# A gated recurrence and a low-rank mixer on one core: another order of the work from the fourth chunk on

## The chip, the cores and the metric

The kernel runs on one core of one Trainium2 chip. The metric is the device time of one execution in microseconds (us). "PE" is TensorE, "PEld" its weight loads, "DVE" VectorE, "ACT" ScalarE, "POOL" GpSimd and "SP" SyncE, which here only starts transfers (DMAs).

## The reference, cut to what matters

The input is q, k, v and a complex gate (a_re, a_im) for 4 batches of 8 heads, 768 steps and 48 channels. A complex state of 48x48 per head is decayed by the gate and takes in the outer product of k and v at each step; q reads its real part. The result, as 768 rows of 384, goes through a mixer over the steps of rank 32 and a two-layer mixer over the channels.

```python
for t in range(S):
    S_re, S_im = ar * S_re - ai * S_im + outer(k[t], v[t]), ar * S_im + ai * S_re
    y[t] = q[t] @ S_re
...
h = x.T @ U @ V
u = x + h.T
out = u + np.maximum(u @ w_ch1, 0.0) @ w_ch2
```

## The kernel before

**Tiles and stages.** Time is cut into chunks of 128 steps: 6 per batch, 24 in all, numbered 0 to 23. Two neighbouring chunks make a group (12 groups). Each chunk goes through these steps, and the names are those of the code and of the profile:

- *gates* (magnitudes, within, totals; L640 to L758): logarithms and exponentials of the gate's size on ACT and DVE, running sums of them on PE ("es ps", "ef ps" at L699 or L705, "tot" at L745 or L751).
- *angles* (turns, waves; L761 to L842): the gate's phase, its running sum on PE ("ph", L806 to L814), sine and cosine ("cs") on ACT.
- *prep* (L850 to L893): DVE multiplies q and k with sizes and phases ("QKC", 768 elements a row), PE transposes them ("tr", L873), ACT copies the result to "QK".
- *levels* (L895 to L972): products of q and k inside the chunk on PE ("inner", first at L923, then the near ones at L920), with scalings of QK on DVE between (L397 is the shared multiply) and masked copies to "DG" (L935). SP then places DG into "AT" by four transfers per chunk (L971).
- *rest* (L973 to L1060): "corners" (L984), the chunk's own key-value product "dk" (L1009), the carried state "G" and "GM" on DVE, and the outputs "y" (L1040 for the part inside the chunk, which reads AT; L1048 for the carried state), copied by ACT to "xo".
- *mixer* (from L1064): for every two chunks of a finished batch, "rank", "mixed", "uTp", then the two layers. The first three pairs use "up" (L1135), later ones "few" (L1235), a scheme with fewer products that needs sums on DVE (L1247, L400); "down" (L1326 and L1369) is the second layer. These are the long products; those of levels and rest are short.

**What sets the order.** The code first records all operations with `plan.add`: the engine, a rank (a stage and a number), what is read and written, and the buffers that are held. Nothing is issued then. Class `Plan`, method `order`, looks up a place in one list for each recorded operation in the table `ORDER`, under its engine and rank, sorts by place, and the operations are then issued in that order. Each engine, and SP's queue too, runs its own operations strictly in this order. Between operations of different engines the list decides nothing: there the semaphores of what is read and written, and of buffers that come free, decide.

Two further tables go with it. `BANKS` holds one letter for each tile in PSUM, in the order in which the tiles are recorded: it names one of four pools ("psT", "psA", "psY", "psM"), each with two buffers. `SPARE` says after which places products without use are issued, each of 128 columns (function `idle`, L1528); there are 91, 72 of them ahead of place 360. No search is part of the file: the tables were made outside it.

Of the kernel before, what the change touches and what calls it, by code (L numbers as in the profile page):

```python
# [30 lines left out]
    "TTTTTTTTTTTTTTTTTTAAAAYYYYTTAAAAYYYYTTAAAAYYYYTTAAAAYYYYTTTTTTTTTTAAAAYYYYTTAAAAYYYTTTMMMMMMTTAAYYAATTMMTTTTMMMMMYMMAMAY"  # L31
    "YYTTMYMMTTTTTTTTTTTTTTTTTTAAATYYMTTTAAAYTYTAYTMMYAAAATYTTTYAAAATYYTTMMTATYYTYAMTTYYYYMYTYYAAMAYYAATATTTAMMAAYMMAYATTAYYM"
    "MTMMAYMMTTTMMTTTAAATTATYATTAYATAYMYYATTTYTAYYTTYMATAYMAYAATYTYTMYAATYYMYMMYYYATYATYATAAATTATYAYAYAYTYATYMYATYMYYAYTTTTAA"
    "TTYMMYYYAAYYTYYYAYYTATYTATATMMAYYATMTAMTMYYYTAYYMMYAYAMYYAMMYTATTTYAYATYTATTTTYATMYMTMTMYYMMTTYATYYMYYTYMATTAAYMAMYYAMA")
# [12 lines left out]
        ('POOL', 'load'): {0: [14], 1: [34], 1.5: [84], 2: [31]},  # L47
        ('DVE', 'load'): {1: [58]},
# [6 lines left out]
        ('ACT', 'gates'): {0: [1, 2, 4, 6, 7, 16, 17, 22, 23, 29, 28, 45, 70, 71], 1: [24, 27, 38, 39, 41, 42, 46, 47, 65, 64, 67, 68], 2: [129, 108,  # L55
# [10 lines left out]
        ('DVE', 'gates'): {0: [5, 8, 13, 18, 19, 54, 49], 1: [30, 21, 40, 43, 44, 51, 50], 2: [111, 143, 156, 185, 169], 4: [277, 322, 323, 372, 356],  # L66
# [10 lines left out]
        ('ACT', 'angles'): {0: [72, 86, 98, 100, 103], 1: [76, 106, 112, 114, 126], 2: [210, 231, 251, 240, 241, 242, 263, 269, 271], 4: [375, 395,  # L77
# [5 lines left out]
        ('DVE', 'angles'): {0: [81, 89], 1: [87, 107], 2: [211, 232, 252], 4: [376, 402, 425], 6: [589, 596, 601, 611, 624, 625, 664], 8: [697, 714,  # L83
# [4 lines left out]
        ('DVE', 'prep'): {0: [85, 104, 110], 1: [121, 128, 145], 2: [226, 250, 265], 3: [203, 304, 309], 4: [373, 424, 427], 5: [443, 470, 472], 6:  # L88
# [1509 lines left out]
```

## Time and profile before

| | |
|---|---|
| median of 3 runs | 621.91 us (621.03 to 622.38) |
| profiled execution, its own time | 619.11 us |
| its span (first to last instruction) | 616.9 us |
| TensorE clock granted, mean | 0.997 |
| busy: PE / DVE / ACT / POOL | 598.9 / 531.5 / 401.8 / 36.3 us |
| PE matmul records | 10,572 |
| moved by DMA | 45.77 MB |

The profile is of one execution. Its first table gives each engine's busy time and its share of the span. A view by stretches gives the same for parts of the span. A view of waits tells for how long an engine sat idle before a line and what released it; "issue" is written where no semaphore explains the idle time. The timeline gives start, duration, engine, line and names, with the idle time before a row in square brackets; neighbouring rows of one line are merged, and a merged row ends when its last result is out, so the next row often starts before that.

### The profile page before, as it was taken

How to read it: one execution, taken by the hardware profiler on the slowest of the kernel's cores; microseconds unless marked ns; L12 is line 12 of the kernel's file. 1: busy time of each engine (PE TensorE's matmuls, PEld its weight loads, DVE VectorE, ACT ScalarE, POOL GpSimd, SP SyncE). 2: the span in 40 equal slices, each digit the busy share in tenths (PEclk: the TensorE clock that was granted, in tenths of full speed). 3: DMA queues.
4: the chain of work that ended last, by engine and by line, in shares of the span. 5: the costliest groups of instructions: out<-in, count | busy, mean ns of one | idle time of the engine just before them, and what ended most of it. 6: DMA issues, size and time to landing. Idle time of an engine off the chain costs nothing.

```text
span 616.9 us, 23966 instructions
## 1 busy us (share of the span) xinstructions
PE 598.9 (97%) x10572; PEld 526.8 (85%) x10572; DVE 531.5 (86%) x967; ACT 401.8 (65%) x789; POOL 36.3 (6%) x76
## 2 busy tenths in 40 slices
PE   6998989999999999999999999999999999999998
PEld 3566767656889979899999999899999998999997
DVE  6999999998999999999999999789889986464554
ACT  6999998989888896886696876565652622202020
POOL 4000000000000010000100100000110000000000
PEclk8999999999999999999999999999999999999999
DMA  9865565644233542521523331700122301000000
GB/s 214 198 148 114 136 133 140 157 126 92 50 57 80 92 85 48 109 54 32 113 49 59 86 70 34 137 9 3 39 54 52 65 9 20 21 7 7 20 20 26
DMA packets 173687, 45.77 MB, mean 74 GB/s; under 512 B 167632, under 2 KB 170384, under 8 KB 173584
## 3 DMA queue, kind: packets, MB, share of 16 engines
q1 hardware_dynamic: 171376, 39.90, 31.4%
q0 software_dynamic: 2208, 4.35, 2.1%
q8 instruction: 83, 1.36, 1.0%
q14 instruction: 20, 0.16, 0.1%
HBM read 33.59 MB, written 4.72 MB: 62 GB/s over the span
## 4 chain that ended last, share of the span: by engine, by line
PE 88%; ACT 8%; issue 1%; DVE 1%; DMA 1%; SPq 0%; ACTq 0%
PE down L1369 25%; PE few L1235 20%; PE up L1135 7%; PE dk L1009 4%; PE tr L873 4%; PE y L1048 3%; PE inner L923 3%; PE down L1326 2%; PE inner L920 2%; ACT gate L394 2%; PE y L1040 2%; PE tot L751 2%; PE mixed L1102 2%; PE rank L1083 1%; PE es ps L699 1%; PE up L1528 1%
## 5 line engine op out<-in xcount | busy, mean ns | idle before, releaser
L397 DVE TENSOR_TENSOR QK<-QK,T 96x512 f32<-96x512 f32 (+2 forms) x144 | 102.3, 725 | 1.5 <-PE corners L984 0.9
L1369 PE MATMUL down<-w,h 128*128 128x192 f32 x396 | 72.3, 330 | 0.0
L394 ACT ACTIVATE gate<-gate 128x768 f32<-128x768 f32 (+1 forms) x82 | 64.7, 795 | 9.3 <-DVE GS L801 5.5
L1369 PEld LDWEIGHTS down<-w,h 128*128 128x128 f32 x396 | 64.5, 190 | 1.3 <-issue 0.7
L884 ACT COPY QK<-tr 96x512 f32<-96x512 f32 x96 | 51.0, 587 | 16.9 <-PE tr L873 16.6
L1243 ACT COPY h<-few 128x512 f32<-128x512 f32 x54 | 31.1, 589 | 46.2 <-PE few L1235 34.3
L1135 PE MATMUL up<-uT,w 128*128 128x256 f32 x216 | 50.4, 385 | 0.0
L400 DVE TENSOR_TENSOR xo<-down,xo 128x192 f32<-128x192 f32 (+1 forms) x79 | 30.1, 384 | 23.1 <-PE down L1369 22.7
L1235 PE MATMUL few<-stage,w 128*128 128x128 f32 x360 | 47.1, 277 | 0.0
L1135 PEld LDWEIGHTS up<-uT,w 128*128 128x128 f32 x216 | 39.9, 190 | 5.5
L1235 PEld LDWEIGHTS few<-stage,w 128*128 128x128 f32 x360 | 44.0, 192 | 0.2
L1247 DVE CUSTOM_DVE_ANT_1 h<-few,h 128x512 f32<-128x512 f32 x54 | 35.9, 684 | 8.4 <-PE few L1235 7.0
L397 DVE TENSOR_TENSOR QKC<-qk,cs 128x768 f32<-128x768 f32 x44 | 41.7, 950 | 1.5 <-PE dk L1009 1.1
L989 ACT COPY AT<-corners 32x128 f32<-32x128 f32 x96 | 24.4, 257 | 24.6 <-PE corners L984 23.3
L1235 PE MATMUL few<-stage,sums 128*128 128x128 f32 x288 | 37.8, 278 | 0.0
L1369 PE MATMUL down<-stage 128*128 128x192 f32 x198 | 37.3, 330 | 0.0
L1235 PEld LDWEIGHTS few<-stage,sums 128*128 128x128 f32 x288 | 34.7, 192 | 0.6
L788 POOL DMA_DIRECT2D gate<-F x15 | 12.0, 799 | 362.6 <-DVE w L587 112.5
L1369 PEld LDWEIGHTS down<-stage 128*128 128x128 f32 x198 | 32.2, 190 | 1.0 <-issue 0.6
L873 PEld LDWEIGHTS tr<-ident,QKC 64*96 64x96 f32 x768 | 24.2, 123 | 10.0 <-issue 3.5
L400 DVE TENSOR_TENSOR h<-few,h 128x512 f32<-128x512 f32 x27 | 18.3, 686 | 16.4 <-PE few L1235 12.4
L873 PE MATMUL tr<-ident,QKC 64*96 64x64 f32 x768 | 29.4, 220 | 2.7 <-DVE QKC L397 1.6
(195 smaller groups left out, 1351.2 us busy)
## 6 DMA issues: line engine op xcount, KB each, us to landing
stage<-in_moe_w_ch_dram SPq DMA_DIRECT2D x12, 768.0 KB, 5.0
qk<-in_q_dram SPq DMA_DIRECT2D x24, 192.0 KB, 3.2
qk<-in_k_dram SPq DMA_DIRECT2D x24, 192.0 KB, 3.8
VP<-in_v_dram SPq DMA_DIRECT2D x24, 192.0 KB, 4.1
gate<-in_a_re_dram SPq DMA_DIRECT2D x22, 192.0 KB, 4.1
gate<-in_a_im_dram SPq DMA_DIRECT2D x22, 192.0 KB, 4.1
AT<-DG SPq DMA_DIRECT2D x96, 32.0 KB, 2.0
T<-E SPq DMA_DIRECT2D x48, 48.0 KB, 3.2
```

What stands on the lines that cost most here:

```text
L394: return nc.scalar.activation(out=o, in_=i, func=f, **kw)
L397: nc.vector.tensor_tensor(out=o, in0=a, in1=b, op=OP.mult)
L400: nc.vector.tensor_tensor(out=o, in0=a, in1=b, op=OP.add)
L873: nc.tensor.transpose(out=get(*ps[r])[0:DQ, h], in_=get(*qkc)[at, h * DQ:(h + 1) * DQ], identity=ident[at, at], tile_position=(r * HC, 0))
L884: nc.scalar.copy(out=to, in_=a)
L989: ACT(0.36, RR, lambda r=r, u=u: nc.scalar.copy(out=get(*ATi).rearrange("p (a u) t -> p a u t", u=2)[r:r + BLK, :, u, BLK:2 * BLK], in_=ge ...
L1009: nc.tensor.matmul(out=get(*dk[r])[x:x + w, h], lhsT=get(*ks)[at, h * DQ + x:h * DQ + x + w], rhs=get(*VPi)[at, h], start=True, stop=True, ...
L1135: nc.tensor.matmul(out=get(*ps)[:, e], lhsT=w1[:, f, (ff + e) * 128:(ff + e + 1) * 128], rhs=get(*uT)[:, f], start=(f == 0), stop=(f == KD ...
L1235: nc.tensor.matmul(out=get(*ps)[:, q], lhsT=w()[:, q * 128:(q + 1) * 128], rhs=v[0](), start=(n == 0 and q == 0), stop=True, skip_group_ch ...
L1243: ACT(c_act(n3 * CH) - 0.045, RU, lambda i=i, k=k: nc.scalar.copy(out=at(i, k), in_=get(*ps)), [ps], [o])
L1247: DVE(c_dve(n3 * CH), RU, lambda i=i, k=k: nc.vector._custom_dve(dve_ops.TENSOR_ADD_SAT, out=at(i, k), in0=get(*ps), in1=at(i, k), s0=math ...
L1369: nc.tensor.matmul(out=get(*to)[:, part], lhsT=x(j), rhs=y[:, j], start=(first and j == 0), stop=(j == KH - 1), skip_group_check=not first)
```

## The change

Only the three tables differ; every recorded operation, its cost figures and the code that issues it are the same. `ORDER` gives other places from 363 on (the fourth chunk, number 3, is then in its *levels*), `BANKS` other pools from about the 53rd tile on, and `SPARE` other places from 436 on, with the same number of products: 19 behind place 360, 91 in all. The tables come from a search that was carried on with transfers reckoned longer than before; the figures it used are not in the file. One line of each table:

```diff
-        25.7: [2222, 2302], 26: [2298], 26.7: [2279, 2381], 27: [2446]},
+        25.7: [2233, 2289], 26: [2298], 26.7: [2340, 2351], 27: [2458]},
...
-         1, 352: 2, 436: 1, 595: 2, 600: 1, 605: 3, 623: 1, 631: 3, 645: 1, 652: 1, 663: 1, 693: 1, 694: 1, 715: 1, 716: 2}
+         1, 352: 2, 438: 1, 585: 3, 600: 2, 609: 1, 618: 3, 621: 1, 651: 1, 655: 1, 680: 1, 693: 1, 704: 1, 724: 1, 726: 2}
```

PE's first other row stands where the span before is at 75.1 us. Three places follow, as the programs have them.

**PE around chunk 4.** First before, from the corners of chunk 3 to the first inner products of chunk 4. "tr" of QKC_93 and QKC_95 are q and k of chunk 4; "y" belongs to chunk 3, and "up<-ident" and "tr<-ident 128x128" are spare products.

```order
L984 MATMUL corners<-QK 32x32 x16
L873 MATMUL tr<-ident,QKC_93 96x64 x16
L1040 MATMUL y<-VP_104,AT_111 64x48 x16
L1528 MATMUL up<-ident 128x128
L873 MATMUL tr<-ident,QKC_95 96x64 x16
L1048 MATMUL y<-GM,QK 64x48 x8
L1048 MATMUL y<-G,QK 64x48 x8
L923 MATMUL inner<-QK 32x48 x32
```

The same stretch of PE after the change:

```order
L984 MATMUL corners<-QK 32x32 x16
L814 MATMUL ph<-F,ident 128x384
L1135 MATMUL up<-uT,w_66 128x256 x6
L873 MATMUL tr<-ident,QKC_93 96x64 x16
L1528 MATMUL tr<-ident 128x128
L873 MATMUL tr<-ident,QKC_95 96x64 x16
L1040 MATMUL y<-VP_104,AT_111 64x48 x16
L1048 MATMUL y<-G,QK 64x48 x8
L1048 MATMUL y<-GM,QK 64x48 x8
L923 MATMUL inner<-QK 32x48 x32
```

A long "up" now stands ahead of the transposes. Before, it stood behind the inner products, between the two halves of "dk" of chunk 4; behind those came this (near inner products of chunk 4, transposes of chunk 5, the next "up"):

```order
L920 MATMUL inner<-QK 16x16 x32
L873 MATMUL tr<-ident,QKC_93 96x64 x16
L873 MATMUL tr<-ident,QKC_95 96x64 x16
L1135 MATMUL up<-uT,w_66 128x256 x6
L984 MATMUL corners<-QK 32x32 x16
```

After the change both halves of "dk" stand together, and this follows them:

```order
L873 MATMUL tr<-ident,QKC_93 96x64 x16
L873 MATMUL tr<-ident,QKC_95 96x64 x16
L920 MATMUL inner<-QK 16x16 x32
L1135 MATMUL up<-uT,w_66 128x256 x6
L923 MATMUL inner<-QK 32x48 x32
```

So no long product is left between the transposes of chunk 4 and the near inner products of chunk 4.

**DVE at the same place.** Before, from the first QKC of chunk 4 to the QK that "inner" of chunk 4 reads (the last row, with T_103); "w_66" is work on the weights.

```order
L397 TENSOR_TENSOR QKC_93<-qk,cs 128x768
L817 SCALAR_TENSOR_TENSOR F<-F,ph 128x384
L400 ISA w_66<-w_66,stage 128x1536
L397 TENSOR_TENSOR QKC_95<-qk,cs 128x768
L397 TENSOR_TENSOR QK<-QK,T_102 96x1024
L397 TENSOR_TENSOR qk<-qk,es 128x768
L397 TENSOR_TENSOR QK<-QK,T_103 96x512
```

After the change:

```order
L397 TENSOR_TENSOR QK<-QK,T_102 96x1024
L817 SCALAR_TENSOR_TENSOR F<-F,ph 128x384
L397 TENSOR_TENSOR QKC_93<-qk,cs 128x768
L397 TENSOR_TENSOR QKC_95<-qk,cs 128x768
L589 SCALAR_TENSOR_TENSOR w_66<-stage,w_66 128x768
L397 TENSOR_TENSOR G<-GM,T_102 96x384
L397 TENSOR_TENSOR QKC_95<-QKC_95,gate 128x768
L397 TENSOR_TENSOR QK<-QK,T_103 96x512
```

The scaling of chunk 3's QK (1024) moved ahead of both QKC, "qk" of chunk 5 and one row of weights were done earlier, and the second use of QKC_95 (for "dk") stands ahead of the last row and no more behind it.

**SP's queue at the same place.** Before, the four placements of chunk 3 (AT_111 from DG_112) stand together:

```order
L728 DMA T_103<-E 48x2x128 x2
L606 DMA V<-UV 32x4x192
L728 DMA T_103<-E 48x2x128
L971 DMA AT_111<-DG_112 32x8x32 x4
L541 DMA gate<-in_a_im_dram 128x8x48 x2
```

After the change:

```order
L728 DMA T_103<-E 48x2x128
L971 DMA AT_111<-DG_112 32x8x32
L541 DMA gate<-in_a_im_dram 128x8x48
L971 DMA AT_111<-DG_112 32x8x32 x2
L550 DMA VP_105<-in_v_dram 128x8x48
L971 DMA AT_111<-DG_112 32x8x32
```

The last placement of chunk 3 now stands behind two loads, of a gate and of v. The later chunks are reordered in the same manner, on all engines.

More of the change, by code (lines that the diff above doesn't have):

```diff
@@ L30 @@
 BANKS = (
[L31 to L34, printed above, removed]
+    "TTTTTTTTTTTTTTTTTTAAAAYYYYTTAAAAYYYYTTAAAAYYYYTTAAAATTMTTTTTTTAMYMMAMAAAMYYYYMMYATTMTTMAMYTAMMMAYATMTMMMAYTYAYAMAAMMAYTY"
@@ L37 @@
+    "ATYYTTMMMAYTTTYYYYTTYAYAYAATYMYTAYATMATTYTTYYTMAMYATAYTYAYYAAMYYTTATAYYAYATYYTTAMAMTAATYYTAATMYTYAYYYAATTMAAYYYTMMATTMYA"
+    "YYMAMMMAYYYMMAYYATTAAYTTAAYYYTMMAMTMMTTMATYAAAYTMAATMYMAAMYATYYMAATMTMAMAAMAATMAATAAYTTYYATYATTYAYAAYYYTTMYYTMTMYYTTTATT"
+    "MYMMMTAYMMMTATYYATYTAATTYAAAMMYTAATTATTTTTMATMTAMMAYYYTYYTAMATYYYAATTYTYYTATAATAYAYTATAAYTTYMYAATMTTYYMMATMTYTMAYAAAYTT")
 ORDER = {
[1 row of a table removed]
[1 row of a table added]
         97], 2.6: [176], 3: [33, 77, 80, 95], 3.5: [61, 60], 5.1: [124], 5.6: [171], 5.7: [125, 214], 6: [212], 6.1: [267], 6.6: [321], 6.7: [196,
[7 rows of a table removed]
[7 rows of a table added]
@@ L47 @@
         ('POOL', 'load'): {0: [14], 1: [34], 1.5: [84], 2: [31]},
         ('DVE', 'load'): {1: [58]},
[6 rows of a table removed]
[6 rows of a table added]
         ('ACT', 'gates'): {0: [1, 2, 4, 6, 7, 16, 17, 22, 23, 29, 28, 45, 70, 71], 1: [24, 27, 38, 39, 41, 42, 46, 47, 65, 64, 67, 68], 2: [129, 108,
         109, 94, 130, 131, 132, 142, 139, 146, 172, 164, 165, 166, 179, 183, 184, 190, 205, 206], 4: [284, 218, 236, 290, 286, 295, 306, 317, 316,
[9 rows of a table removed]
-        ('DVE', 'gates'): {0: [5, 8, 13, 18, 19, 54, 49], 1: [30, 21, 40, 43, 44, 51, 50], 2: [111, 143, 156, 185, 169], 4: [277, 322, 323, 372, 356],
[10 rows of a table removed]
@@ L77 @@
-        ('ACT', 'angles'): {0: [72, 86, 98, 100, 103], 1: [76, 106, 112, 114, 126], 2: [210, 231, 251, 240, 241, 242, 263, 269, 271], 4: [375, 395,
[5 rows of a table removed]
-        ('DVE', 'angles'): {0: [81, 89], 1: [87, 107], 2: [211, 232, 252], 4: [376, 402, 425], 6: [589, 596, 601, 611, 624, 625, 664], 8: [697, 714,
[4 rows of a table removed]
-        ('DVE', 'prep'): {0: [85, 104, 110], 1: [121, 128, 145], 2: [226, 250, 265], 3: [203, 304, 309], 4: [373, 424, 427], 5: [443, 470, 472], 6:
[6 rows of a table removed]
-        ('ACT', 'prep'): {0: [115, 117, 120, 122], 1: [158, 147, 154, 160], 2: [266, 270, 283, 281], 3: [319, 320, 327, 318], 4: [442, 439, 446, 445],
[4 rows of a table removed]
@@ L100 @@
-        ('DVE', 'rest'): {0: [118, 149, 155, 175, 159, 170, 194], 1: [174, 229, 234, 259, 209, 235, 248, 253], 2: [288, 315, 325, 366, 291, 314, 324,
[8 rows of a table removed]
-        ('DVE', 'levels'): {0: [123, 135, 148, 136, 137, 152], 1: [177, 192, 202, 195, 198, 225], 2: [292, 302, 308, 301, 303, 312], 3: [328, 371,
[9 rows of a table removed]
-        ('ACT', 'levels'): {0: [138], 1: [215], 2: [305], 3: [378], 4: [468], 5: [530], 6: [764], 7: [830], 8: [962], 9: [1058], 10: [1175], 11:
[14 rows of a table removed]
-        ('ACT', 'rest'): {0: [191, 182, 200, 201, 219, 223, 222], 1: [255, 261, 256, 258, 280, 279, 278], 2: [342, 341, 336, 335, 385, 390, 391], 3:
[10 rows of a table removed]
@@ L145 @@
-        ('ACT', 'small'): {0: [594, 285, 307, 492, 396, 554, 590, 549, 622, 635], 1: [742, 800, 775, 808, 780, 844, 860], 2: [900, 930, 1065, 1076,
[4 rows of a table removed]
-        ('DVE', 'small'): {0: [246, 599, 630, 636, 639, 637, 684, 681, 602, 606, 729, 735], 1: [703, 739, 689, 832, 877, 897, 862, 919, 901, 938, 978,
[29 rows of a table removed]
-        ('POOL', 'small'): {0: [929, 793], 1: [1101, 1103, 1208], 2: [1514, 1246, 1421], 3: [1726, 1584, 1640], 4: [1867, 1831, 1915], 5: [2198, 1951,
-        2151], 6: [2186, 2266, 2321], 7: [2424, 2353, 2486], 8: [2581, 2503, 2566], 9: [2655, 2617, 2651], 10: [2710, 2678, 2761]},
@@ L182 @@
-        ('POOL', 'angles'): {6: [614], 8: [706, 731], 10: [866, 912], 12: [1057], 14: [1265, 1312], 16: [1448, 1521], 18: [1698], 20: [1950, 2023],
-        22: [2175, 2244]},
-        ('DVE', 'mixing'): {3: [842, 845, 1024, 1078, 1098, 933, 1062, 1026, 1243, 1250, 1268, 1316, 1280]},
[9 rows of a table added]
+        ('DVE', 'gates'): {0: [5, 8, 13, 18, 19, 54, 49], 1: [30, 21, 40, 43, 44, 51, 50], 2: [111, 143, 156, 185, 169], 4: [277, 322, 323, 377, 356],
[10 rows of a table added]
+        ('ACT', 'angles'): {0: [72, 86, 98, 100, 103], 1: [76, 106, 112, 114, 126], 2: [210, 231, 251, 240, 241, 242, 263, 269, 271], 4: [378, 398,
[5 rows of a table added]
@@ new lines @@
+        ('DVE', 'angles'): {0: [81, 89], 1: [87, 107], 2: [211, 232, 252], 4: [385, 401, 423], 6: [580, 581, 584, 591, 616, 617, 627], 8: [698, 720,
[4 rows of a table added]
+        ('DVE', 'prep'): {0: [85, 104, 110], 1: [121, 128, 145], 2: [226, 250, 265], 3: [203, 304, 309], 4: [372, 424, 427], 5: [395, 460, 464], 6:
[6 rows of a table added]
+        ('ACT', 'prep'): {0: [115, 117, 120, 122], 1: [158, 147, 154, 160], 2: [266, 270, 283, 281], 3: [319, 320, 327, 318], 4: [435, 436, 444, 446],
[4 rows of a table added]
+        ('DVE', 'rest'): {0: [118, 149, 155, 175, 159, 170, 194], 1: [174, 229, 234, 259, 209, 235, 248, 253], 2: [288, 315, 325, 362, 291, 314, 324,
[8 rows of a table added]
@@ new lines @@
+        ('DVE', 'levels'): {0: [123, 135, 148, 136, 137, 152], 1: [177, 192, 202, 195, 198, 225], 2: [292, 302, 308, 301, 303, 312], 3: [328, 369,
[9 rows of a table added]
+        ('ACT', 'levels'): {0: [138], 1: [215], 2: [305], 3: [376], 4: [466], 5: [508], 6: [770], 7: [837], 8: [959], 9: [1026], 10: [1176], 11:
[14 rows of a table added]
+        ('ACT', 'rest'): {0: [191, 182, 200, 201, 219, 223, 222], 1: [255, 261, 256, 258, 280, 279, 278], 2: [342, 341, 336, 335, 425, 393, 388], 3:
[10 rows of a table added]
+        ('ACT', 'small'): {0: [593, 285, 307, 432, 394, 494, 558, 510, 620, 624], 1: [705, 811, 793, 785, 799, 838, 850], 2: [933, 865, 1045, 1059,
[4 rows of a table added]
@@ new lines @@
+        ('DVE', 'small'): {0: [246, 601, 632, 630, 643, 667, 642, 637, 664, 614, 765, 735], 1: [681, 710, 641, 823, 831, 868, 894, 900, 899, 938, 978,
[29 rows of a table added]
+        ('POOL', 'small'): {0: [969, 1046], 1: [1152, 1144, 1225], 2: [1329, 1374, 1480], 3: [1738, 1530, 1531], 4: [1794, 1736, 1894], 5: [2230,
+        1983, 2191], 6: [2392, 2151, 2339], 7: [2442, 2396, 2429], 8: [2552, 2665, 2666], 9: [2633, 2602, 2709], 10: [2757, 2699, 2701]},
+        ('POOL', 'angles'): {6: [615], 8: [699, 749], 10: [846, 930], 12: [1071], 14: [1266, 1322], 16: [1457, 1526], 18: [1712], 20: [1950, 2007],
@@ L185 @@
+        22: [2214, 2291]},
+        ('DVE', 'mixing'): {3: [646, 1022, 691, 1028, 1035, 652, 1076, 1094, 1102, 1222, 1260, 1290, 1264]},
 }
 SPARE = {20: 8, 32: 9, 62: 1, 66: 1, 73: 1, 82: 5, 91: 1, 113: 6, 116: 1, 119: 8, 140: 8, 153: 6, 157: 4, 167: 1, 168: 1, 207: 6, 216: 1, 217: 1, 282:
-         1, 352: 2, 436: 1, 595: 2, 600: 1, 605: 3, 623: 1, 631: 3, 645: 1, 652: 1, 663: 1, 693: 1, 694: 1, 715: 1, 716: 2}
+         1, 352: 2, 438: 1, 585: 3, 600: 2, 609: 1, 618: 3, 621: 1, 651: 1, 655: 1, 680: 1, 693: 1, 704: 1, 724: 1, 726: 2}
```

252 rows, old and new, of the table ORDER are left out of this document.

## The prediction

> **What bounds the kernel now.** I read the page first, then the view by stretches, the view of waits, and the timeline of TensorE and VectorE where PE waits. The page's first table has PE at 97%:
>
> ```profile
> PE 598.9 (97%) x10572; PEld 526.8 (85%) x10572; DVE 531.5 (86%) x967; ACT 401.8 (65%) x789; POOL 36.3 (6%) x76
> ```
>
> Of the 18.0 us that PE lacks in a span of 616.9, the part ahead of the first moved row (75.1 us) is the same in both kernels. By stretches (columns: PE, PEld, DVE, ACT, POOL busy, granted clock, DMA share, GB/s):
>
> ```profile
> 0.00:75.00 75.00, 66.37 (x1246) 45.31 (x1246) 68.74 (x123) 68.06 (x132) 6.44 (x29) 0.98 0.73 166
> 75.00:100.00 25.00, 21.41 (x586) 16.28 (x582) 23.83 (x38) 24.06 (x44) 0.00 (x0) 1.00 0.47 108
> 100.00:140.00 40.00, 39.48 (x551) 26.94 (x538) 36.90 (x58) 34.99 (x64) 0.96 (x1) 1.00 0.62 151
> 140.00:400.00 260.00, 257.77 (x5108) 232.59 (x5107) 248.22 (x437) 201.79 (x397) 17.18 (x26) 1.00 0.38 73
> ```
>
> The first 75 us hold 8.6 of the 18.0, and they stay. From 75 to 100 PE lacks 3.6, from 100 to 140 0.5, from 140 to 400 2.2. Behind 400 there is only the tail of about 3 us. So another order can win idle time of some 6 us, plus what the products themselves cost in another order. DVE is busy 23.8 of 25 and 248.2 of 260: it is the second bound, and an order that crowds it makes PE wait. PE's waits from 75 us to the end:
>
> ```profile
> PE inner L920 <- issue: 1.3, 1, 1.3
> PE dk L1009 <- issue: 1.3, 2, 0.8
> PE tr L873 <- DVE QKC L397: 0.8, 1, 0.8
> PE y L1048 <- DVE QK L397: 0.5, 1, 0.5
> PE inner L923 <- ACT xo L1057: 0.4, 1, 0.4
> PE inner L923 <- ACT F L394: 0.4, 1, 0.4
> PE tr L873 <- issue: 0.4, 1, 0.4
> ```
>
> Two kinds: waits for VectorE or ScalarE, nearly all before 97 us, and four waits with no releaser ("issue"), 3.0 us together. None is for a transfer.
>
> **The waits without a releaser** fall inside runs of short products. Two of them, with the rows around:
>
> ```profile
> 93.84 0.61 PE L920 MATMUL inner<-QK 96*16 96x16 f32 x55
> 95.77 0.24 PE L920 MATMUL inner<-QK 96*16 96x16 f32 x9 [1.31 <-issue]
> 95.94 1.14 PE L873 MATMUL tr<-ident,QKC 64*96 64x64 f32 x32
> ...
> 227.11 0.65 PE L873 MATMUL tr<-ident,QKC 64*96 64x64 f32 x16
> 229.37 0.91 PE L1009 MATMUL dk<-VP,QKC 64*64 64x48 f32 x47
> 231.06 0.45 PE L1009 MATMUL dk<-VP,QKC 64*48 64x48 f32 x17 [0.78 <-issue]
> ```
>
> Counted in the trace (loads, products and semaphore instructions of PE), the waits stand at PE's instructions 3,520, 7,617, 8,128 and 13,248: whole multiples of 256 apart, but for one instruction. And one DMA queue brings 83 pieces:
>
> ```profile
> q8 instruction: 83, 1.36, 1.0%
> ```
>
> 1.36 MB in 83 pieces is 16 KB each, and PE's 21,300 instructions in 83 pieces are 256 each. So I read these waits as the next 256 instructions arriving late. At 231.06 PE had run through 256 instructions since 227.11, 3.9 us with the wait, 3.2 without; the other boundaries that I counted with 3.6 us or more of work between them show none, unless the piece came late (5.9 us at 95.77). A stretch of 256 instructions that holds only short products is at risk, and the order decides where the boundaries fall.
>
> [...]
>
> **The change, term by term.** The sum is made against the profiled execution (619.11 us, span 616.9); the median of the runs is 621.91, 2.8 more, and I put the difference onto the median.
>
> *1. Switches between shapes.* Nothing is removed or added; the same products run. But a row costs more when a product with another layout follows:
>
> ```profile
> 99.80 0.46 PE L984 MATMUL corners<-QK 96*32 96x32 f32 x32
> 100.07 0.93 PE L923 MATMUL inner<-QK 96*32 96x48 f32 x64
> ...
> 109.20 0.46 PE L984 MATMUL corners<-QK 96*32 96x32 f32 x32
> 109.59 1.13 PE L1009 MATMUL dk<-VP,QKC 64*64 64x48 f32 x32
> ```
>
> From start to start, corners take 0.27 us ahead of inner and 0.39 ahead of dk: 0.12 for the switch; in the same way I find 0.10 to 0.18 for the other rows. Counted in the two orders behind 75 us, neighbouring blocks differ in layout 210 times before and 200 times now. 10 x 0.14 = **-1.4 us** (-1.0 to -1.8).
>
> *2. From 75 to 97 us, chunk 4.* PE before:
>
> ```profile
> 84.04 0.26 PE L873 MATMUL tr<-ident,QKC 64*96 64x64 f32 x1 [0.79 <-DVE QKC L397]
> 84.50 0.65 PE L873 MATMUL tr<-ident,QKC 64*96 64x64 f32 x15 [0.21 <-DVE F L817]
> 87.37 0.67 PE L1048 MATMUL y<-GM,QK 96*64 96x48 f32 x16 [0.48 <-DVE QK L397]
> 88.94 0.89 PE L923 MATMUL inner<-QK 96*32 96x48 f32 x64 [0.42 <-ACT xo L1057]
> 90.45 2.86 PE L1135 MATMUL up<-uT,w 128*128 128x256 f32 x12
> ```
>
> With the 1.31 above and 0.21 at 78.1 the idle times are 3.4; from start to start, against equal rows elsewhere (near inner: 2.10 from 93.84 to 95.94), they cost 4.0. VectorE meanwhile works without a gap:
>
> ```profile
> 87.24 0.95 DVE L397 TENSOR_TENSOR qk<-qk,es 128x768 f32<-128x768 f32 x1
> 88.11 0.68 DVE L397 TENSOR_TENSOR QK<-QK,T 96x512 f32<-96x512 f32 x1
> 88.71 0.95 DVE L397 TENSOR_TENSOR QKC<-QKC,gate 128x768 f32<-128x768 f32 x1
> ```
>
> The new order puts the "up" of 2.8 us ahead of the transposes, so PE works while VectorE catches up: the waits of 0.79, 0.21 and most of 0.48 go. VectorE's rows in the new order reach the QK for inner 0.4 later (0.95 for the second QKC now ahead, 0.54 for a G row now behind), about 89.1. PE with "up" done is there at about 88.6: 0.5 is late. Next late: two QKC of chunk 5 and the DG copies, four rows of 0.9 and three short ones after that, against 2.4 us of inner, dk and tr: 1.5 more. So VectorE keeps PE back 2.0 instead of 2.5. The boundary at 3,520 lies inside the near inner again, and the one before it inside the first inner of chunk 4, each now behind a stretch of 2.5 us of short products. VectorE's waits stretch these to some 3.3; I take 0.6 for both on top. 2.0 + 0.6 - 4.0 = **-1.4 us** (from -2.0, no boundary late, to +2.0, both as late as at 95.77).
>
> *3. Boundaries behind 140 us.* Before, three waits: 0.35, 0.78, 0.52, together 1.65. In the new order I count four stretches of 256 with under 3 us of work: at 8,128 (dk of chunk 10, as before), 11,456 (dk of chunk 14), 12,224 and 14,016 (near inner of chunks 14 and 16). 4 x 0.66 (between the mean of these three, 0.55, and of all four, 0.74) - 1.65 = **+1.0 us** (-1.65, all hidden, to +3.6, four times 1.31). [...]
>
> *4. Transfers and the rest.* SP's queue shows the changed risk: the last placement of chunk 3 now waits behind two loads. The rows for a placement, and for its landing:
>
> ```profile
> L971 SPq DMA_DIRECT2D AT<-DG x96: 585/608/2046, 35.0 to 510.6; - x96
> AT<-DG SPq DMA_DIRECT2D x96, 32.0 KB, 2.0
> ```
>
> Six starts of 0.61 and 2.0 to land are 5.7 us from the last DG copy (about 78.5) or the T transfers (80): 85.7. PE reaches the "y" that reads it at 87.1: covered by 1.4 us; if a start takes 2.05, the cover is gone. Counted by places in the new order, six placements (chunks 19, 22 and 23) have under 3 us of PE's products between the last release in the queue and their reader; before, none had under 4.8. Loads of q, k and gates keep 2.9 or more. Bounds: -0.4 (the one wait for F at 170 us goes) to +4 (four placements 1 us late); the nearest row is that no wait of PE before was for a transfer, so I take **+0.4 us**.
>
> Sum: -1.4 - 1.4 + 1.0 + 0.4 = -1.4. 619.11 would become 617.7, and the median 621.91 - 1.4 = **620.5 us**.
>
> **The rivals.**
> (a) *No boundary is late.* The DMA share behind 140 us is 0.38 against 0.62 earlier, which speaks for timely pieces; that two of the waits before were at this share speaks against. Terms 2 and 3 then are -2.0 and -1.65: 621.91 - 1.4 - 2.0 - 1.65 + 0.4 = 617.3. [...]
> (b) *The waits only move*: VectorE has the same 531.5 us, with no idle time in its rows from 84 to 94 (some stand above), and later stretches are just as full. What PE no longer waits for at chunk 4 comes back at the next crowded place (VectorE's rows behind "up" to 128 us put PE 0.8 further back). Switches -1.4, early gain given back, boundaries and transfers +1.4: 621.9. This is also the outcome if an order changes nothing.
> (c) *Slower: instruction pieces arrive late where short products were pushed together.* Six stretches have under 3 us of work now, before four had up to 3.2. A piece as late as the one before 95.77 (5.9 us between boundaries) costs 3 us where 2.9 us of work lie between. Two such (chunk 4, where the DMA share is 0.47 to 0.62, has both candidates) and four of 0.9 are 9.6, before 3.0: +6.6, less the switches, 1.4, and 0.5 of VectorE: 621.91 + 4.7 = 626.6. It decides as soon as more than about 1.4 us is lost beyond term 2 and 3. One late placement of AT at chunks 19 or 22 adds 1 each.
>
> **How the numbers follow.** The forecast at 620.5 has a chance of 0.36, (a) 0.09, (b) 0.22, (c) and its milder forms 0.33. What a measurement of this kernel can tell from no change is about 0.2%, 1.24 us. The forecast spreads by about 1.5 us around its sum, so 0.33 of its 0.36 and (a) count as faster: 0.42. Same: (b) and 0.03, so 0.25. Slower: 0.33. The best ends of all terms make 616.0, the worst 630.5; leaving out the far ends, one in ten each, the range is 617.0 to 626.5.
>
> **What would show it.** PE's rows between 82 and 97 us without the waits for QKC, "up" starting near 84, and the second "up" near 95 instead of 97.0: term 2. Waits named "issue" inside inner or dk of chunks 4, 10, 14 and 16, more than three behind 140 us: term 3. A PE busy time about 1.4 us below 598.9: term 1. Waits of "y" at L1040 for DG transfers, at chunks 3, 19, 22 or 23: term 4 was too small. The prediction is wrong if VectorE shows new idle time before 300 us while PE waits for it just after, which none of my sums holds.

## The result and the profile after

The changed kernel took **619.43 us** (median of 5 runs, 618.60 to 619.51), and the kernel before, run beside it, 621.52 (5 runs, 620.67 to 622.38): a ratio of 0.9968, 95% interval 0.9955 to 0.9981, so 0.32% faster. The forecast was 620.5, with a range from 617.0 to 626.5. Run twice more beside before, on two chips, the changed kernel took 619.25 and 619.29, and before 619.74 and 619.71: ratios of 0.9990 (0.9971 to 1.0009) and 0.9991 (0.9978 to 1.0003). So it takes the same time in all three places; before took 2 us more in the first, and no trace shows why (its profiled execution there, 619.11 us, was faster than every timed run). What the change is worth lies between nothing and 0.3%. The runs below take this apart into a gain and a loss of 3 to 4 us each.

The profiled execution took 619.34 us with a span of 617.6. By the same stretches as before (columns: PE, PEld, DVE, ACT, POOL busy, granted clock, DMA share, GB/s):

```profile
0.00:75.00 75.00, 66.38 (x1214) 44.92 (x1214) 68.30 (x123) 67.59 (x130) 6.33 (x29) 1.00 0.71 164
75.00:100.00 25.00, 20.81 (x575) 16.04 (x574) 21.32 (x34) 21.57 (x41) 0.00 (x0) 0.91 0.34 82
100.00:140.00 40.00, 39.29 (x552) 28.16 (x551) 37.13 (x60) 35.51 (x64) 0.96 (x1) 0.97 0.62 141
140.00:400.00 260.00, 258.87 (x5114) 233.49 (x5114) 249.12 (x438) 203.83 (x401) 17.10 (x26) 1.00 0.38 75
```

The first 75 us are as before. From 75 to 100 PE lacks 4.2 us where it lacked 3.6, and the granted clock, 1.00 before, is 0.91. From 140 to 400 PE lacks 1.1 where it lacked 2.2. PE's waits from 75 us on (in all, times, longest):

```profile
PE inner L923 <- issue: 2.9, 1, 2.9
PE dk L1009 <- issue: 0.7, 1, 0.7
PE tr L873 <- DVE QK L397: 0.7, 1, 0.7
PE mixed L1102 <- DVE h L1179: 0.6, 1, 0.6
PE y L1040 <- ACT QK L884: 0.4, 1, 0.4
PE tr L873 <- DVE QKC L397: 0.3, 1, 0.3
```

Two waits at instruction boundaries are left of four, but one is now 2.9 us. It stands in chunk 4, and PE's rows around it show what follows:

```profile
83.75 2.75 PE L1135 MATMUL up<-uT,w 128*128 128x256 f32 x12
86.43 0.65 PE L873 MATMUL tr<-ident,QKC 64*96 64x64 f32 x16
...
88.51 0.78 PE L1040 MATMUL y<-VP,AT 64*64 64x48 f32 x32 [0.42 <-ACT QK L884]
...
90.29 0.80 PE L923 MATMUL inner<-QK 96*32 96x48 f32 x56
93.97 0.29 PE L923 MATMUL inner<-QK 96*32 96x48 f32 x8 [2.88 <-issue]
94.19 1.14 PE L1009 MATMUL dk<-VP,QKC 64*64 64x48 f32 x64
95.26 1.09 PE L873 MATMUL tr<-ident,QKC 64*96 64x64 f32 x16
97.02 1.09 PE L873 MATMUL tr<-ident,QKC 64*96 64x64 f32 x16 [0.66 <-DVE QK L397]
```

"Up" starts near 84 and VectorE's waits of 0.79 and 0.21 are gone, as forecast. But after 56 products of the first "inner" the next instructions are missing, and 16 transposes that take 0.65 us at 86.43 take 1.09 at 95.26: the clock records of the trace show 0.5 from 95.3 us for 6.8 us. Before has none between 12 us and the tail at 616.

Why is the piece late? By the count of PE's instructions, PE passed the boundary before it (number 3,008) at 87.7; the 256 instructions behind that boundary end where the wait of 2.88 us stands. SP's row, and the DMA traffic from 86 to 96 us in 40 slices of 0.25:

```profile
88.03 0.37 SPq L569 DMA_DIRECT2D stage<-in_moe_w_ch_dram  x1
```
```profile
DMA  0000000000009665999999600000000000003000
GB/s 0 0 0 0 0 0 0 0 0 0 0 0 160 135 135 209 344 418 393 430 418 369 234 0 0 0 0 0 0 0 0 0 0 0 0 0 66 0 33 0
```

A load of weights, 768 KB, starts to move at 89.0 and keeps the DMA engines half busy or more until 91.7; the trace's DMA records put the piece of instructions at 91.68 to 92.70, at its very end, and PE goes on at 93.97. In the kernel before the same load was issued 0.9 us later, at 88.92. A piece was late there too: PE passed its boundary (3,264) at 89.85, the load's bytes moved from 90.7 to 93.9, and the piece started at 93.38, 3.5 us behind the boundary, against 4.0 in after. But PE needed 4.4 us to run through those 256 instructions, which held a long "up", and only 3.2 in after, where "up" now stands ahead of them. So a delay of much the same length made a wait of 1.31 us before and of 2.88 after.

### The profile page after: what moved, and what is told of

It reads as the page before. It is cut to its first block, busy times and chain, and to the rows that moved or that the text cites. A ratio compares the mean times of both kernels' runs of the same rounds, so it can differ in the third digit from the quotient of the medians.

```text
span 617.6 us, 23926 instructions
## 1 busy us (share of the span) xinstructions
PE 599.9 (97%) x10570; PEld 529.2 (86%) x10570; DVE 530.8 (86%) x967; ACT 402.4 (65%) x789; POOL 36.4 (6%) x76
## 3 DMA queue, kind: packets, MB, share of 16 engines
q8 instruction: 83, 1.36, 0.9%
## 4 chain that ended last, share of the span: by engine, by line
PE 83%; ACT 7%; DVE 5%; DMA 2%; issue 2%; SPq 2%; DVEq 0%; ACTq 0%
PE down L1369 25%; PE few L1235 20%; PE up L1135 6%; PE tr L873 4%; PE dk L1009 4%; PE y L1048 3%; PE inner L923 3%; ACT gate L394 2%; PE inner L920 2%; PE y L1040 2%; PE tot L751 2%; PE mixed L1102 1%; PE up L1528 1%; PE corners L984 1%; DVE QK L397 1%
## 5 line engine op out<-in xcount | busy, mean ns | idle before, releaser
L884 ACT COPY QK<-tr 96x512 f32<-96x512 f32 x96 | 51.5, 586 | 13.7 <-PE tr L873 13.3
L1135 PEld LDWEIGHTS up<-uT,w 128*128 128x128 f32 x216 | 41.6, 196 | 6.3
```

The source lines that it names most:

```text
L884: nc.scalar.copy(out=to, in_=a)
L1135: nc.tensor.matmul(out=get(*ps)[:, e], lhsT=w1[:, f, (ff + e) * 128:(ff + e + 1) * 128], rhs=get(*uT)[:, f], start=(f == 0), stop=(f == KD ...
```

## The experiments

**Theory A**: the new order gains behind chunk 5 (fewer switches, fewer boundaries that wait) and loses in chunk 4, where a piece of instructions falls behind a weight load and the wait for it halves the clock. **Rivals**: the late waits belong to rows and not to boundaries (C); the load has nothing to do with it (D, F); the gain is in chunk 4, where VectorE holds PE back less (G); after is 0.32% faster wherever it runs (E); B and H are named with their runs. Three sets of four kernels ran, each set on one chip beside before, which took 619.38, 619.74 and 619.71 us there. The table has them in this order, four rows to a set:

| run | us, median (lowest to highest) | ratio to before of its set (95%) |
|---|---|---|
| before_again | 619.22 (618.10 to 621.93) | 1.0002 (0.9985 to 1.0019) |
| after_shift128 | 629.59 (628.33 to 630.45) | 1.0159 (1.0139 to 1.0179) |
| after_cutload | 615.13 (613.99 to 616.35) | 0.9928 (0.9908 to 0.9948) |
| before_cutload | 618.59 (617.14 to 620.91) | 0.9992 (0.9978 to 1.0007) |
| after_again | 619.25 (614.11 to 621.06) | 0.9990 (0.9971 to 1.0009) |
| after_split | 616.28 (613.50 to 620.35) | 0.9947 (0.9927 to 0.9967) |
| early_before | 615.93 (614.73 to 618.60) | 0.9941 (0.9920 to 0.9962) |
| early_after | 625.57 (621.71 to 626.70) | 1.0084 (1.0060 to 1.0108) |
| after_third | 619.29 (617.48 to 620.69) | 0.9991 (0.9978 to 1.0003) |
| after_shift24 | 619.87 (618.21 to 621.15) | 0.9998 (0.9983 to 1.0012) |
| after_shift64 | 615.12 (614.84 to 616.76) | 0.9933 (0.9921 to 0.9945) |
| early_before_split | 614.63 (613.51 to 615.70) | 0.9918 (0.9905 to 0.9932) |

**Before, profiled again** (no edit).

> The kernel before, unchanged, profiled once more, since its first profiled execution (619.11 us) lies under all of its timed runs (620.67 to 622.38) and so may not show where a usual run's time goes. Theory A (instruction pieces, and what a long wait for one does): a usual run of before has a wait without releaser near 95.8 us that is longer than the 1.31 us of the first profile, 2 us or more, and behind it the granted clock at 0.5 for some microseconds, as after has it at 93.97 us; 621 to 622 us. Rival B (the difference of 2 us lies elsewhere, in the first 75 us or spread over many rows): the wait near 95.8 us is again about 1.3 us, the clock does not fall, and the same stretches by window differ elsewhere. Ratio to before 1.000.

Rival B was right here, and my guess of a long wait in before's usual run wrong. PE's rows of this execution (618.83 us, span 616.7):

```profile
94.00 0.61 PE L920 MATMUL inner<-QK 96*16 96x16 f32 x55
95.84 0.24 PE L920 MATMUL inner<-QK 96*16 96x16 f32 x9 [1.23 <-issue]
96.01 1.15 PE L873 MATMUL tr<-ident,QKC 64*96 64x64 f32 x32
```

A wait of 1.23 us, and the 32 transposes behind it take 1.15 us (1.14 in the first profile), with a granted clock of 1.00 from 75 to 140 us. So before's chunk 4 costs what its first profile showed.

**The boundaries moved.** The first of three runs on after that only add PE instructions at the very start:

```
-    begun, run, at = set(), 0, 0
+    begun, run, at, early = set(), 0, 0, [32]
...
+        while early[0]:
+            early[0] -= 1
+            nc.tensor.matmul(out=to[:, 0:16], lhsT=ident, rhs=ident[:, 0:16], start=True, stop=True)
```

> After, with 32 products of 16 columns added to the first spare product, while PE has nothing to do (3.6 us idle before 8.80 us): 128 more PE instructions ahead of everything else, so that every boundary of 256 instructions falls 128 instructions earlier in the program; order, tiles and all other engines are as in after. Theory A: the waits without a releaser belong to the boundaries, so those at 93.97 (2.9 us) and 312.36 us (0.7) go or change, and others come at rows that had none. By the stretches of 256 in after's trace, boundaries with under 3.7 us of work between them are then more and shorter (about 6.6 us short in all, before 1.1), so PE's waits named issue grow to 4 to 8 us behind 75 us, and the time is 621 to 627 us. Rival C (the waits belong to the rows themselves, or to an engine the profile does not show): the two waits stay where they are and the time is 619.4 within 0.4.

The time, 629.59, is 3 us over what I expected, for a reason of my own making: the added products were not free.

```profile
2.86 13.67 PE L1532 MATMUL tr<-ident 128*128 128x16 f32 x64
```

Each product is two such rows and loads 128 columns of weights to multiply 16, ahead of the record of a clock of 1.0 (it begins at 21.8 us, in after at 13.3; there, six spare rows of 128x384 take 3.78 us ahead of it, at 1.42, and 1.99 behind it, at 27.50). A row takes 0.21 us. "Up" of chunk 4 starts at 93.73 where it started at 83.75, so 10.0 us are lost ahead of chunk 4, and only 1.1 of the 11.1 us in the span behind it. The waits themselves answer the question:

```profile
PE dk L1009 <- issue: 2.6, 3, 1.6
PE tr L873 <- issue: 1.3, 1, 1.3
...
PE down L1369 <- issue: 0.5, 1, 0.5
```

The old two (inner of chunk 4, dk of chunk 14) are gone and five new ones have come, at PE instructions 3,520, 5,312, 6,336, 6,848 and 7,872: multiples of 256 apart again, at rows that had no wait 128 instructions earlier. Rival C falls. In after's trace these are the five stretches with the least work if one counts from 16 instructions ahead of a boundary to the next one: 2.2 to 2.9 us.

**The load taken away**, in after and in before (the second weight matrix is then partly left out):

```
-                out=get("raw", p)[:, at:end].rearrange("p (c m) two -> p c (m two)", c=a.shape[1]), in_=a.bitcast(U32)),
+                out=get("raw", p)[:, at:end].rearrange("p (c m) two -> p c (m two)", c=a.shape[1])[:, 0:1, 0:64],
+                in_=a.bitcast(U32)[:, 0:1, 0:64]) if p == 7 else nc.sync.dma_start(
+                out=get("raw", p)[:, at:end].rearrange("p (c m) two -> p c (m two)", c=a.shape[1]), in_=a.bitcast(U32)),
```

> After, in which the one weight load that SP issues at 88.03 us (768 KB) brings only 32 KB; the rest of the staged weights is what lay there, so part of the second weight matrix is left out. Theory A: PE's wait of 2.88 us at 93.97 is a piece of 16 KB of instructions that stood behind this load (it started 91.68, with the load's bytes moving from about 89 to 92), and the clock of 0.5 behind it comes from that wait. Without the load the piece starts about 1 us behind the boundary at 87.7, the wait is under 0.7, the clock stays at 1.0 and the time falls by 3 to 6 us, to 613.5 to 616.5. Rival D (the stretch of instructions is too short in itself, the load does not matter): the wait stays above 2 us and the time within 0.5 of 619.4.

Measured 615.13, some 4.2 under before on the same chip and under after in the other sets. PE's rows (line numbers are two further on):

```profile
91.92 0.29 PE L925 MATMUL inner<-QK 96*32 96x48 f32 x8 [0.95 <-issue]
92.14 1.14 PE L1011 MATMUL dk<-VP,QKC 64*64 64x48 f32 x64
93.22 0.65 PE L875 MATMUL tr<-ident,QKC 64*96 64x64 f32 x16
94.53 0.65 PE L875 MATMUL tr<-ident,QKC 64*96 64x64 f32 x16 [0.67 <-ACT QK L886]
```

The wait falls from 2.88 to 0.95 (I had said under 0.7), and the transposes take 0.65 again, with the clock at 1.0 to the end. The piece started 1.9 us behind the boundary, not 1. The span is 613.0: 4.6 less than after's, of which 1.9 is the wait and 2.7 PE's busy time (597.2 against 599.9), which goes with the half clock. Rival D falls.

> Before with the same load cut to 32 KB (here issued at 88.92 us), part of the second weight matrix left out in the same way. Theory A: the wait at 95.77 (1.31 us in the first profile, more in a usual run) falls under 0.5, and the time by what that wait and its clock cost in a usual run, 1 to 6 us, to 615.5 to 620.5; what then stands between this and the cut after is the worth of the new order without this accident. Rival D: within 0.5 of 621.5.

618.59 against 619.38: the interval holds 1, so no more than the lower end of what I expected, about the 1.3 us of the wait at most. In the profile the wait near 95 us is gone, as theory A said (the piece started at 92.1, 1.1 us behind its boundary). In before this load costs little. With the load cut in both, the new order takes 615.13 and the old one 618.59 on the same chip: without this accident the new order is worth 3.5 us.

**The load in three transfers**, on after, with all of the work done (o_ and i_ are the two sides of the old transfer):

```
+                cuts = ((0, 0, 128), (0, 128, 768), (1, 0, 768)) if p == 7 else ((None, 0, o_.shape[2]),)
+                for c, lo_, hi_ in cuts:
+                    cs_ = slice(None) if c is None else slice(c, c + 1)
+                    nc.sync.dma_start(out=o_[:, cs_, lo_:hi_], in_=i_[:, cs_, lo_:hi_])
```

> After, in which the weight load issued at 88.03 us goes out as three transfers of 64, 320 and 384 KB, so the whole work is done and the bulk of the bytes starts some 0.6 us later. Theory A: the piece of instructions asked for near 88.7 us now finds a shorter queue ahead of it; the wait at 93.97 falls from 2.88 us to 1 to 2, the clock stays at 1.0 if the wait stays under some 1.4 us, and the time falls by 1 to 4 us against after on the same chip. Rival F (the piece waits for the whole burst whatever its cut): the wait stays at 2.5 us or more, the clock falls again, and the time is that of after within 0.5.

616.28, 3.0 under after on the same chip. In the profiled execution (span 613.4) the piece started 1.9 us behind the boundary, as without the load, the wait was 1.1 and the clock stayed at 1.0. (The 1.4 us of the expectation lies between 1.31, with a clock of 1.0 behind it in before, and 1.58, with 0.5 in after_shift128.) By the DMA records the piece now moved amid the load's bytes (90.27 to 91.52, the bytes of the two large transfers from 90.1 to 93.7) and no more at their end. Rival F falls. Some runs still took 618 to 620 us.

**Halves of the order exchanged.** The places of all operations were renumbered: the first 585 as they follow in one kernel, the rest as in the other, pools and spare products with them. The line for "up" in chunk 4 of early_before, as an example (462, 490, 569 and 509 are before's places, the rest nearly after's):

```
-        ('PE', 'mixing'): {0: [300, 431, 326, 474, 538, 491, 638, 644, 651, 702, 724, 764, ...
+        ('PE', 'mixing'): {0: [300, 462, 326, 490, 569, 509, 639, 645, 652, 702, 724, 764, ...
```

> The first 585 operations in the order and with the tiles' pools of before (up to the end of chunk 5's work, about 106 us), all others in the order and with the pools of after. Theory A: the gain of the new order lies behind 106 us (fewer switches, fewer waits at boundaries: 1.4 and 1.0 to 1.5 us), and its loss lies in chunk 4 (the late piece). So this order has the gain without the loss: PE's busy time about 1.4 under before's 598.9, waits named issue behind 140 us under 1 us, no half clock behind 95 us, 615.5 to 617.5 us, faster than both. Rival G (the gain lies in chunk 4, where VectorE no longer keeps PE waiting, as term 2 of the prediction has it): the time is that of before, within 0.6.

615.93 us: 3.8 under before and 3.3 under after on the same chip. Its stretches from 75 and from 140 us:

```profile
75.00:100.00 25.00, 22.24 (x651) 17.11 (x647) 24.65 (x41) 24.41 (x47) 0.00 (x0) 1.00 0.53 126
140.00:400.00 260.00, 259.15 (x5117) 234.13 (x5116) 248.64 (x443) 202.82 (x398) 17.09 (x26) 1.00 0.39 76
```

PE lacks 0.85 us from 140 to 400 where it lacked 2.2, its busy time is 597.3 in all (before 598.9), and its only waits for instructions behind 75 us are 0.5 and 0.4. So the new order's gain lies behind chunk 5, and rival G falls. Not all of the 3.8 is that gain: of the 3.9 us that the span is shorter than before's, 0.8 lies between 75 and 100 us, where the order is still that of before and only the wait near 95 us is shorter (0.5, in before's two profiles 1.3 and 1.2). Some 3 us are left for the part behind.

> The reverse: the first 585 operations as in after, the others as in before. Theory A: the late piece and the half clock of chunk 4 (2.9 and about 2.7 us) without the later gain: 2 to 4 us over before, 621.4 to 623.5 us on this chip, PE busy 600.5 to 602. Rival G: VectorE's waits of chunk 4 are gone and that is the gain, so this takes 0.5 to 2 us less than before.

625.57, slower as expected and by 2 us more. The two exchanges do not add up: here the early part of the new order costs 5.8 us and the late part is worth 6.3, where early_before gave 3.3 and 3.8. The joint itself adds waits (PE waits 1.5 us for ScalarE's rw, 1.4 for its QK, 0.9 for a placement of AT), and the profiled execution was the fastest of its runs (621.71), so what the others lost is not shown. The profile is worth a look all the same, because chunk 4 in after's order was not caught in it:

```profile
91.55 0.29 PE L923 MATMUL inner<-QK 96*32 96x48 f32 x8 [0.20 <-issue]
94.86 0.65 PE L873 MATMUL tr<-ident,QKC 64*96 64x64 f32 x16 [1.36 <-ACT QK L884]
```

PE passed the boundary at 88.0 and SP issued the load at 88.35, 0.3 us behind it as in after. But the piece started at 88.78, ahead of the load's first bytes at 89.37, so the wait is 0.20 and there is no half clock. Whether the piece falls behind the load can thus go either way with the same order: here it started 0.6 us ahead of the load's first bytes, in after 2.6 us behind them (89.07 to 91.68). This is not what I had expected of this run.

**After once more, and small shifts.** These used weights of 16 columns:

```
+            nc.tensor.matmul(out=to[0:16, 0:16], lhsT=ident[:, 0:16], rhs=ident[:, 0:16], start=True, stop=True)
```

> After, unchanged, beside before on the same chip. On this chip before took 619.2 to 619.4 us in the runs so far, 2 us less than in the runs that gave the ratio of 0.9968. Theory A: every run of after pays the late piece at chunk 4 and half the clock behind it; by the profiled executions (before 616.7 and 616.9 us of span, after 617.6) after would take 0.7 to 0.9 us more than a good run of before: 619 to 620.2 us, a ratio of 0.999 to 1.002 here. Rival E (after is 0.32% faster wherever it runs, and what the two profiles show of before is not its usual run): 617.0 to 617.8 us.

> After, unchanged, once more beside before on the same chip, as the base of the three runs below. Theory A: 619 to 620, with the wait of 2.9 us at chunk 4 and the half clock behind it, and a ratio to before between 0.996 and 1.002. Rival E (the first ratio of 0.9968 is what the change is worth): 0.995 to 0.998 again.

Both within what theory A said; both profiles have the wait of 2.9 us and the clock at 0.5 for 6.8 us. One run of the first took 614.11, near the 615.1 of after without its late piece (after_cutload, after_shift64); no profile shows that run. Rival E does not hold for these two chips, if narrowly (the intervals begin at 0.9971 and 0.9978).

> After, with 6 products of 16x16 (weights of 16 columns, so that they are short) in the first spare product: 24 PE instructions more ahead of everything, nothing else. Theory A: the boundary in chunk 4 is passed 0.7 us earlier (at 87.0 in after's time instead of 87.7), so its piece of instructions is asked for before the weight load's bytes (SP issues at 88.03, they move from about 89). The wait of 2.9 us and the half clock go; stretches of 256 with 2.9 to 3.2 us of work then stand at three other places and cost about 0.8 us. 613.5 to 616 us, 4 to 5 under after on the same chip. Rival F (24 instructions make no difference, the piece waits for the load all the same): within 0.6 of after.

A miss: 619.87, a wait of 3.3 us, the piece at 91.15 as if nothing had been done. My lead was counted with 1 us from boundary to piece, and cutload had shown 1.9: 24 instructions put the boundary at about 86.3 here, 1.9 later is 88.2, and by then the load is on its way (issued at 87.42, first bytes at 88.4).

> The same with 16 such products: 64 PE instructions. Theory A, with the rule read from the run with 128 instructions more (the five stretches with under 2.9 us of work, counted from 16 instructions ahead of the boundary, were the five that waited, and each waited about 3.3 us less its work): chunk 4 is free as with 24, but eight stretches, at PE instructions 8,896, 10,176, 11,968, 13,248, 13,760, 17,088, 18,624 and 19,392, have 2.5 to 3.2 us of work and cost about 3.7 us in all: 616 to 618.5 us, with waits named issue near 244, 275, 322, 367, 491 and 506 us of after's time. Rival C (waits belong to rows): within 0.6 of after, with the waits where after has them.

615.12, 4.2 under after on the same chip, and 1 us better than I expected. The piece came at 86.94, ahead of the load, and chunk 4 has no wait for instructions:

```profile
89.84 0.89 PE L923 MATMUL inner<-QK 96*32 96x48 f32 x64
90.65 1.14 PE L1009 MATMUL dk<-VP,QKC 64*64 64x48 f32 x64
91.73 0.65 PE L873 MATMUL tr<-ident,QKC 64*96 64x64 f32 x16
94.14 0.65 PE L873 MATMUL tr<-ident,QKC 64*96 64x64 f32 x16 [1.77 <-ACT QK L884]
```

Part of what was won shows up as a wait for ScalarE. Of the eight stretches that I named only two lost time (from start to start 0.3 us at 11,968 and 1.1 at 18,624; the view of waits lists the second alone, with 0.9), so the rule "3.3 us less the work" asks too much: six stretches with 2.5 to 3.2 us of work were fed in time. What sets the moment at which a piece is asked for stays open.

> The order of before for the first 585 operations, the new order behind, and the weight load of 768 KB of chunk 4 (issued at 88.9 us there) as three transfers. Theory A: of what is left in chunk 4 only the wait near 95 us (0.5 in the profile of the unsplit order, 1.2 to 1.3 in before) can shrink: 0 to 0.8 us under the unsplit order, 615 to 616. Rival H (three transfers interleave with the piece longer than one): 0.5 to 2 us over it.

614.63, the fastest of all, 0.8% under before. Its wait near 95 us is no longer listed; two short waits for placements of AT (0.7 us together) are new. The sets differ, so what the split adds over early_before (615.93) is not measured by itself.

## Why the prediction came out right, step by step

The time fell inside the range and the sign of the medians was right, but by luck: two of the four terms were wrong, in opposite directions. In profiled executions:

- **Term 1, switches (-1.4): right in sign, and if anything too small.** PE's busy time without the half clock is 597.2 to 597.3 (after_cutload, early_before), before it was 598.9: -1.6. Counted only from the "y" row at 75 us on, just ahead of the first moved row, before and its two other profiles read 533.0 to 533.4, and the four runs with the new order behind chunk 5 and no half clock (these two and the two with the load in three transfers) 530.4 to 531.2: -1.8 to -3.0. That the ten switches are the reason is not shown: no run changed them alone. In after itself the busy time reads 599.9, because the half clock hides the gain.
- **Term 2, chunk 4 (-1.4): wrong.** The VectorE part came only beside the late piece. What PE lacks from 75 to 100 us, less the waits for instructions, went from 3.6 - 1.3 = 2.3 to 4.2 - 2.9 = 1.3 (forecast: to 2.0, from 2.5 in the text and 2.7 in its sum). But it is 1.5 in after_cutload, 2.0 in early_after and 2.4 in after_shift64, where the waits for the piece are 0.95, 0.2 and none. The sooner the piece comes, the longer PE then waits ahead of the second transposes of chunk 5, for ScalarE's QK by the view: 0.67, 1.36 and 1.77 us. So without the late piece little of this gain is left, and rival (b), that the waits only move, holds in this place. The step that failed is "I take 0.6 for both on top". I named the right boundary (inside the first inner of chunk 4), but it cost 2.9, because I checked the stretch for its work and not for what the DMA engines carry when its piece is asked for; and no term held the clock, which took another 1.5 to 2.7 (PE busy 598.7 to 599.9 in three executions against 597.2). With the end at +2.0 for "both as late as at 95.77", the bound was too tight as well. The second "up" came at 98.7, not near 95. By the first of the exchanges the early part of the new order costs 3.3 us.
- **Term 3, boundaries behind 140 us (+1.0): wrong in sign.** Only one of the four that I counted waited (11,456, 0.7); 8,128, 12,224 and 14,016 did not, and PE lacks 1.1 less there. The step that failed is "four stretches of 256 with under 3 us of work", counted from the moment PE crosses a boundary. By the DMA records the piece for 14,016 started at 369.39, while PE crossed 13,760 at 370.2, inside a run of long "few" products; the piece for 11,456 started 1.0 us behind the crossing, which lay in short transposes. So a piece can start ahead of PE's crossing, here with long rows in front of the boundary. Rival (a), no boundary late, is what nearly happened here; with it the term is -1.65.
- **Term 4, transfers (+0.4): too large.** No wait of PE behind 75 us was for a transfer in after's three profiles.

So -1.6 - 1.0 - 1.1 and + 1.6 (the wait in chunk 4) + 2.7 (the clock) make +0.6, and the spans are 616.9 and 617.6 (0.5 of that 0.7 lies ahead of the first moved row). The profiled pair thus goes the other way than the medians, because before's profiled execution was faster than each of its timed runs. The forecast of -1.4 against the medians, where -2.1 and twice -0.4 to -0.5 was measured, agrees by cancellation: by early_before the rest of the new order gave 3.8 (some 3 of it behind chunk 5) where terms 1 and 3 together gave 0.4, and chunk 4 took 3.3 where term 2 gave 1.4. Rival (c), a piece late in chunk 4, was the mechanism there; its price of 3 us for such a piece was right for the wait and left out the clock. The sign that I named as proof against my sums came too. VectorE was idle because PE's late piece held back what it reads, and PE then waited 0.66 us for VectorE. Only the idle time is a consequence of the late piece: PE's wait is as long or longer where the piece came sooner (above), and none of my sums held it. VectorE's row in after:

```profile
94.33 0.69 DVE L397 TENSOR_TENSOR QK<-QK,T 96x512 f32<-96x512 f32 x1 [2.65 <-PE inner L923]
```

Of some 70 boundaries of 256 instructions behind 75 us, four show a wait in before and two in after; the one behind a weight load cost 4.6 us of span, its clock included, against the run with that load cut (617.6 and 613.0).

## What to carry to other kernels

Where a long unrolled program keeps one engine busy, look for its waits without a releaser, find the instruction count at which they fall, and see what large transfer is under way when the next piece is due: cutting that transfer in three, or moving the count by 64 instructions, gave 3 to 4 us here, while moving it by 24 gave nothing. When a new order changes little, run each half of it with the other half of the old order; here that turned "nothing" into -3.8 and +3.3, and the better half alone beat both kernels (0.9941, and 0.9918 with the load in three transfers). Run both exchanges: the other one gave larger figures, so the halves are not independent.

## What the runs showed of the hardware

- Behind 75 us, a wait of PE was followed by a granted clock of 0.5 when it lasted 1.6 us (after_shift128, at 103.6) or 2.9 to 3.3 us (after, after_shift24), for 6.8 us; behind waits of 0.95 to 1.31 us (before and five of the runs) and of 1.36 and 1.48 us (early_after) the clock stayed at 1.0. Behind the 1.77 us of after_shift64 it was 0.5 for 3.4. The records of 0.5 are 3.413 us long in before (at 8.7 us) and 6.827 us in after (at 95.3).
- PE went on 1.2 to 1.6 us after the last byte of a late piece, at every wait named "issue" behind 75 us in all fourteen profiles; for example 94.34 to 95.77 in before, 92.70 to 93.97 and 310.96 to 312.36 in after.
- With the load in one transfer the piece came at the end of the load's bytes in after's profiles (91.68 against 91.7); with the load in three it came amid them (90.27, the bytes of the two large transfers from 90.1 to 93.7).
- At the start of the kernel, ahead of the first clock record of 1.0 in both, 32 rows of products with 16 columns of weights took 1.04 us in all (after_shift64), and 64 rows with 128 columns 13.67 (after_shift128), for 16 columns of data each.
